# Attention of the later token blocks: two chunks a stop, inside an output pass, through the free h bank

## The chip, the cores and the metric

One core of one Trainium2 chip. The metric is the device time of one execution in microseconds (us). The engines go by the profile's names: PE (TensorE), DVE (VectorE), ACT (ScalarE), POOL (GpSimd), SP (SyncE, which issues the DMAs). PEld is PE's weight load.

## The reference

Attention with decay runs over blocks of 64 rows and carries a state; its output is the input of two MLPs in a row, each a product, a non-linear function and a second product.

```python
for b in range(nb):                       # 12 blocks of 64 rows
    intra = einsum('bhic,bhjc->bhij', qb, kb) * Dmask      # lam**(i-j), below the diagonal
    intra = einsum('bhij,bhjd->bhid', intra, vb)
    inter = einsum('bhid,bhde->bhie', qb * lam_pow, kv_state)
    out[:, :, sl] = intra + inter
    kv_state = lam_block * kv_state + einsum('bhsd,bhse->bhde', kb * rev_pow, vb)
# x = out as 1536 tokens x 512
x = elu(x @ w_in) @ w_out                 # d_ff = 2048, first MLP ("layer 0")
h = x @ w_in2; g = P(h) / (Q(h) + 1e-6)   # P cubic, Q = 1 + |b0||h| + |b1|h*h
y = g @ w_out2                            # second MLP ("layer 1")
```

The shapes are 2 batches, 8 heads, 768 rows, 64 columns a head.

## The kernel before, in words

The 1536 tokens are three token blocks t of 512, and each layer runs over them with d_ff in 16 steps f of 128. A step has an h pass (`mlp_h`, 12 matmuls of 128x512 at L435 into a PSUM bank of the pool `ph`, which has two) and, two steps later, a y pass (`mlp_y`, 12 matmuls at L517 into the four y banks of `py`). The 12 are three parts of four: high weights by high data, high weights by low data, low weights by high data. Between h and y stand the ELU's operations: ACT L448 and L449, DVE L450 (which is the last to read the h bank), ACT L452 (high part) and DVE L453 (low part). PSUM has eight banks: two `pa`, two `ph`, four `py`.

During t = 0 of layer 0 the weights of later steps are made from raw bits as well: DVE L78, L81 and L84 (1024 wide) put a weight tile together, ACT L127 rounds it to its high part and DVE L128 makes the low part. The raw tiles come by DMA (SP L122, L114).

The attention of the first 512 rows is done in the opening. Chunks 8 to 23, 64 rows of each of the 8 heads (4 pairs m), belong to token blocks 1 and 2 and are worked off in stops, 9 during t = 0 and 8 during t = 1 (the table `visits`), each between an h pass and the y pass that follows. At a stop (`att_visit`) `sm_products(n, d)` issues for the new chunk n the products of keys and queries (L340, into half 0 of bank `aa0`), and for the chunk before, d, the products of masked scores and values (L345, into `aa1`), of keys and values (L351, into half 1 of `aa0`) and of queries and state (L356, into `aa1`). All are 64x64, two for each pair m. Behind them: DVE L376 masks the scores of n, POOL L371 decays its queries (256 wide), ACT L384 copies the output of d to `xr`, DVE L388 adds the state (ACT L386 for a batch's first chunk), and in the step after ACT decays the state (L395, four operations) and the keys (L365, four). The powers of the decay for one chunk are made at the first stop (PE L333, ACT L335). The keys and values of a chunk are loaded by four DMAs (L323) and queries and keys of two chunks by two (L308).

In this part the program's order is written by hand (`manual_schedule`): every engine works its instructions in the order in which the loop over the steps emits them. From t = 2 on a scheduler orders them.

Of the kernel before, what the change touches and what calls it, by code (L numbers as in the profile page):

```python
# [8 lines left out]
F32 = mybir.dt.float32  # L9
# [7 lines left out]
P = 128  # L17
T = 512
# [11 lines left out]
def fused_kernel(ctx, tc, lam, qkv, w1, w2, ab, out):  # L30
# [16 lines left out]
    ph = ctx.enter_context(tc.tile_pool(name="ph", bufs=2, space=PSUM))  # L47
# [252 lines left out]
    aa_tiles = []  # L300

    def sm_load_qk(k):

        c, row = k // 2, 4 * P
        qk = qq.tile([P, NP, 2, C], F32, tag="qk", name=f"qk{c}")
        src = qkv[c, 0, 0]
        for rho, r in enumerate(ROWS):
            nc.sync.dma_start(  # L308
                out=qk[r].rearrange("p (g a) x i -> p g (a x i)", a=2),
                in_=bass.AP(src.tensor, src.offset + (1 - rho) * D * row,  # L310
                            [[row, D], [2 * P * row, NP // 2], [1, row]]))
# [15 lines left out]
    def sm_products(n, d):  # L327

        if not aa_tiles:
            aa_tiles.extend(pa.tile([P, T], F32, tag=f"pa{i}", name=f"aa{i}")  # L330
                            .rearrange("p (x m i) -> p x m i", x=2, m=NP) for i in range(2))
            for r in ROWS:
                nc.tensor.matmul(aa_tiles[1][r, 1], lhsT=pick[r], rhs=mask64[r, :, 1:CS + 1],  # L333
                                 start=True, stop=True, skip_group_check=True)
            nc.scalar.activation(out=qpow[:, :, 0:CS], in_=aa_tiles[1][:, 1], func=AF.Copy)  # L335
        pn, pd = chunk.get(n), chunk.get(d)
        for m in range(NP):
            if pn:
                for r in ROWS:
                    nc.tensor.matmul(aa_tiles[0][r, 0, m], lhsT=pn["k"][r, m],  # L340
                                     rhs=pn["q"][r, m], start=True, stop=True,
                                     skip_group_check=True)
            if pd:
                for i, r in enumerate(ROWS):
                    nc.tensor.matmul(aa_tiles[1][ROWS[1 - i], 0, m], lhsT=pd["kv"][r, m, 1],  # L345
                                     rhs=pd["s"][r, m], start=m == 0, stop=d % KB == 0,
                                     skip_group_check=True)
        for m in range(NP):
            if pd and d % KB < KB - 1:
                for r in ROWS:  # L350
                    nc.tensor.matmul(aa_tiles[0][r, 1, m], lhsT=pd["kv"][r, m, 0],  # L351
                                     rhs=pd["kv"][r, m, 1], start=True, stop=True,
                                     skip_group_check=True)
            if pd and d % KB:
                for i, r in enumerate(ROWS):
                    nc.tensor.matmul(aa_tiles[1][ROWS[1 - i], 0, m], lhsT=state[r, m, 0],  # L356
                                     rhs=pd["q"][r, m], start=False, stop=True,
                                     skip_group_check=True)

    def sm_decay_k(n):  # L360

        kv = chunk[n]["kv"]
        if n % KB < KB - 1:
            for m in range(NP):
                nc.scalar.activation(out=kv[:, m, 0], in_=kv[:, m, 0], func=AF.Copy,  # L365
                                     scale=mask64[:, m, CS - 1:CS])

    def sm_decay_q(n):
        q = chunk[n]["q"]
        if n % KB:  # L370
            nc.gpsimd.tensor_tensor(out=q, in0=q, in1=qpow[:, :, 0:CS], op=ALU.mult)  # L371

    def sm_mask(n):
        b = chunk[n]
        b["s"] = s = ap_.tile([P, NP, CS], F32, tag="s", name=f"s{n}")
        nc.vector.tensor_tensor(out=s, in0=aa_tiles[0][:, 0], in1=mask64[:, :, 0:CS], op=ALU.mult)  # L376

    def sm_out(d):

        t, js = d * CS // T, slice(d * CS % T, d * CS % T + CS)  # L380
        if t not in xraw:
            xraw[t] = xr.tile([P, NP, T], F32, tag="xr", name=f"xr{t}")
        first, last = d % KB == 0, d % KB == KB - 1
        nc.scalar.activation(out=xraw[t][:, :, js], in_=aa_tiles[1][:, 0], func=AF.Copy)  # L384
        if first:
            nc.scalar.activation(out=state[:, :, 0], in_=aa_tiles[0][:, 1], func=AF.Copy)  # L386
        elif not last:
            nc.vector.tensor_tensor(out=state[:, :, 0], in0=aa_tiles[0][:, 1],  # L388
                                    in1=state[:, :, 1], op=ALU.add)

    def sm_decay_state(d):

        if d % KB not in (0, KB - 1):
            for m in range(NP):
                nc.scalar.activation(out=state[:, m, 1], in_=state[:, m, 0], func=AF.Copy,  # L395
                                     scale=qpow[:, m, CS - 1:CS])

# [102 lines left out]
    def mlp_y(layer, t, f):  # L500
# [27 lines left out]
    with ExitStack() as actx:  # L528
# [4 lines left out]
        qq = actx.enter_context(tc.tile_pool(name="qq", bufs=2))  # L533

# [20 lines left out]
        dmask = ac.tile([P, H, C + 1], F32, name="dmask")  # L555
        qpow = ac.tile([P, NP, C], F32, name="qpow")
        state = ac.tile([P, NP, 2, D], F32, name="state")

        mask64 = dmask.rearrange("p (m h) i -> p m h i", h=2)[:, :, 1, CS:]
# [8 lines left out]
        def make_qpow():  # L568
# [5 lines left out]
            def double(n):  # L574
# [4 lines left out]
        yy, hh = ((py, "y"),) * 2, ((ph, "h"),) * 2  # L579
        pp = (yy, hh, yy, yy, hh, yy, yy, ((ph, "h"), (pa, "pa0")))  # L580
# [4 lines left out]
        loads = [[(sm_load_qk, first), (sm_load_kv, first)], [(sm_load_kv, first + 1)],  # L585
                 [(sm_load_qk, first + 2)]]
        loads += [[(sm_load_kv, k + 1)] + [(sm_load_qk, k + 2)] * (k % 2 == 0 and k + 2 < end)
                  for k in range(first + 1, end - 1)]
        with tc.manual_schedule():
# [17 lines left out]
            for load, k in loads.pop(0):  # L607
                load(k)
# [43 lines left out]
            for h in range(5, H):  # L652
# [45 lines left out]
            nc.gpsimd.tensor_copy(  # L698
                out=mask64[ROWS[1]],
                in_=dmask.rearrange("p (m h) i -> p m h i", h=2)[ROWS[1], :, 0, 0:CS + 1])  # L700
# [3 lines left out]
        h_pool = lambda: (ph, "h")  # L704
# [8 lines left out]
        def att_visit(due, more):  # L713

            n = todo.pop(0) if more and todo else None
            d = due.pop() if due else None
            sm_products(n, d)
            if n is not None:
                sm_mask(n)
                sm_decay_q(n)  # L720
                due.append(n)
            if d is not None:
                sm_out(d)
                del chunk[d]

        with tc.manual_schedule():
            due = []
            next_d = []
# [6 lines left out]
            visits = [(3, 5, 7, 9, 10, 12, 13, 14, 15), (2, 4, 6, 8, 10, 12, 14, 15)]  # L735
            assert sum(park_at.values()) == len(parks)
            for layer, t, f in steps(0, 0) + steps(0, 1):
                if f == 0 and t:
# [3 lines left out]
                    for n in due:  # L742
                        sm_decay_k(n)
                new = mlp_h(layer, t, f, later=True)
                queue.append((layer, t, f))
                if t or f != 1:
                    run(old, 2)
                    for d in next_d:
                        sm_decay_state(d)
                    next_d = []  # L750
# [27 lines left out]
                if f in visits[t]:  # L778
                    att_visit(due, t == 0 or f < NF - 1)
                    next_d = list(due)  # L780
                    for n in due:
                        if f < NF - 1:
                            sm_decay_k(n)
# [9 lines left out]
                if loads and (f in visits[t][1 - t:] or t == 0 and f in (1, 2)):  # L793
                    for load, k in loads.pop(0):
                        load(k)
# [3 lines left out]
                if len(queue) > LAG:  # L799
                    mlp_y(*queue.pop(0))  # L800
# [10 lines left out]
    def h_pool():  # L811
        nh[0] += 1
        return ((ph, "h"), (ph, "h"), (pa, "pa0"), (pa, "pa1"))[nh[0] % 4]
# [89 lines left out]
```

## Time and profile before

| | us |
|---|---|
| median of three runs | 572.01 (571.96 to 572.03) |
| the profiled execution | 572.56 |
| its span, first to last instruction | 570.8 |
| PE busy | 564.6 (99%) |
| DVE busy | 464.7 (81%) |
| ACT busy | 358.5 (63%) |
| POOL busy | 29.8 (5%) |

The profiled execution lies 0.55 us above the median, and 1.8 us of it lie outside the span. PE is busy from end to end, so its column says little by itself. What is to be read is the chain of work that ended last, which gives the price of each pass and each stop, and the other engines' timelines in the stretch of the stops: which of them runs how far behind PE.

### The profile page before, as it was taken

How to read it: one execution, taken by the hardware profiler on the slowest of the kernel's cores; microseconds unless marked ns; L12 is line 12 of the kernel's file. 1: busy time of each engine (PE TensorE's matmuls, PEld its weight loads, DVE VectorE, ACT ScalarE, POOL GpSimd, SP SyncE). 2: the span in 40 equal slices, each digit the busy share in tenths (PEclk: the TensorE clock that was granted, in tenths of full speed). 3: DMA queues.
4: the chain of work that ended last, by engine and by line, in shares of the span. 5: the costliest groups of instructions: out<-in, count | busy, mean ns of one | idle time of the engine just before them, and what ended most of it. 6: DMA issues, size and time to landing. Idle time of an engine off the chain costs nothing.

```text
span 570.8 us, 9255 instructions
## 1 busy us (share of the span) xinstructions
PE 564.6 (99%) x3550; PEld 464.9 (81%) x3550; DVE 464.7 (81%) x722; ACT 358.5 (63%) x690; POOL 29.8 (5%) x51
## 2 busy tenths in 40 slices
PE   8999999999999999999999999999999999999997
PEld 7877888888888888888888888888888888888885
DVE  6999999965676635877979999888898888898882
ACT  3746646875554545555568976667877666776672
POOL 7401001100100000000000000000000000000000
PEclk9999999999999999999999999999999999999999
DMA  8977677464687513434432500000400000200001
GB/s 291 318 225 243 237 227 214 107 206 128 204 240 229 165 49 136 167 135 177 150 108 78 182 3 1 1 2 0 145 3 2 0 1 0 75 0 1 1 1 74
DMA packets 41215, 64.58 MB, mean 113 GB/s; under 512 B 20178, under 2 KB 20178, under 8 KB 41170
## 3 DMA queue, kind: packets, MB, share of 16 engines
q1 hardware_dynamic: 41168, 63.98, 35.8%
q8 instruction: 28, 0.46, 0.3%
q14 instruction: 17, 0.14, 0.1%
q10 hardware_dynamic: 2, 0.00, 0.0%
HBM read 53.48 MB, written 10.49 MB: 112 GB/s over the span
## 4 chain that ended last, share of the span: by engine, by line
PE 98%; DMA 1%; SPq 0%; ACT 0%; issue 0%
PE h L435 46%; PE y L517 43%; PE y L426 3%; PE aa L340 1%; DMA att<-qkv_in 1%; PE aa L351 1%; PE pa L243 1%; PE pa L209 1%; PE pa L249 0%; PE aa L356 0%; PE aa L345 0%; SPq L192 0%; PE sums L256 0%; PE pa L291 0%; ACT o L487 0%; PE aa L333 0%
## 5 line engine op out<-in xcount | busy, mean ns | idle before, releaser
L435 PE MATMUL h<-xhi,w 128*128 128x512 f32 x768 | 204.8, 389 | 0.0
L517 PE MATMUL y<-ghi,w 128*128 128x512 f32 x712 | 191.8, 392 | 0.0
L435 PEld LDWEIGHTS h<-xhi,w 128*128 128x128 f32 x768 | 143.8, 188 | 30.3 <-DVE w L128 0.4
L517 PEld LDWEIGHTS y<-ghi,w 128*128 128x128 f32 x712 | 132.3, 188 | 27.8
L435 PE MATMUL h<-xlo,w 128*128 128x512 f32 x384 | 102.6, 389 | 0.0
L517 PE MATMUL y<-glo,w 128*128 128x512 f32 x356 | 95.3, 389 | 0.0
L435 PEld LDWEIGHTS h<-xlo,w 128*128 128x128 f32 x384 | 72.1, 188 | 15.0
L517 PEld LDWEIGHTS y<-glo,w 128*128 128x128 f32 x356 | 66.8, 188 | 14.2
L461 ACT ACTIVATE a<-h,babs 128x512 f32<-128x512 f32 x48 | 33.0, 688 | 63.8 <-PE h L435 63.8
L448 ACT ACTIVATE a<-h 128x512 f32<-128x512 f32 x48 | 28.3, 589 | 43.1 <-PE h L435 42.9
L465 DVE SCALAR_TENSOR_TENSOR b<-b,babs,a 128x512 f32<-128x512 f32 x48 | 36.0, 751 | 20.9 <-ACT b L462 20.7
L450 DVE SCALAR_TENSOR_TENSOR b<-a,h 128x512 f32<-128x512 f32 x48 | 32.7, 681 | 15.3 <-ACT a L449 12.1
L452 ACT ACTIVATE ghi<-b 128x512 fp32r<-128x512 f32 x48 | 30.0, 626 | 22.4 <-DVE b L450 22.4
L453 DVE TENSOR_TENSOR glo<-b,ghi 128x512 fp32r<-128x512 f32 x48 | 34.0, 709 | 7.0 <-ACT ghi L452 4.8
L463 ACT ACTIVATE p<-h,cab 128x512 f32<-128x512 f32 x48 | 37.7, 785 | 0.0
L467 ACT ACTIVATE a<-b,one 128x512 f32<-128x512 f32 x48 | 35.0, 729 | 3.1 <-DVE b L465 2.6
L469 DVE SCALAR_TENSOR_TENSOR p<-p,cab,h 128x512 f32<-128x512 f32 x48 | 35.8, 746 | 1.2
L473 DVE SCALAR_TENSOR_TENSOR b<-b,one,a 128x512 f32<-128x512 f32 x48 | 35.8, 746 | 0.1
L475 DVE SCALAR_TENSOR_TENSOR p<-p,cab,a 128x512 f32<-128x512 f32 x48 | 35.8, 746 | 0.0
L58 DVE TENSOR_TENSOR glo<-p,ghi 128x512 fp32r<-128x512 f32 x48 | 33.0, 688 | 3.0 <-PE y L426 1.5
L468 DVE TENSOR_TENSOR p<-p,h 128x512 f32<-128x512 f32 x48 | 32.8, 682 | 2.9 <-ACT p L463 2.9
L477 DVE SCALAR_TENSOR_TENSOR p<-b,p 128x512 f32<-128x512 f32 x48 | 33.1, 690 | 1.2
(88 smaller groups left out, 611.2 us busy)
## 6 DMA issues: line engine op xcount, KB each, us to landing
raw<-w_in SPq DMA_DIRECT2D x64, 512.0 KB, 4.5
att<-qkv_in SPq DMA_DIRECT2D x16, 256.0 KB, 6.0
qk<-qkv_in SPq DMA_DIRECT2D x16, 256.0 KB, 4.3
kv<-qkv_in SPq DMA_DIRECT2D x64, 64.0 KB, 4.0
w2d<-wbuf SPq DMA_DIRECT2D x16, 256.0 KB, 4.5
wbuf<-w2d SPq DMA_DIRECT2D x16, 256.0 KB, 2.8
x2d<-o SPq DMA_DIRECT2D x12, 256.0 KB, 2.3
x2r<-x2d SPq DMA_DIRECT2D x12, 256.0 KB, 3.1
```

The costliest lines, as they stand in the source:

```text
L58: lo_eng.tensor_tensor(out=lo, in0=src, in1=hi.bitcast(F32), op=ALU.subtract)
L435: nc.tensor.matmul(h, lhsT=w[:, a, 0, k * P:(k + 1) * P], rhs=xs[layer, t, k][b], start=i == k == 0, stop=i == 2 and k == NP - 1)
L453: lambda: nc.vector.tensor_tensor(out=glo, in0=b, in1=ghi.bitcast(F32), op=ALU.subtract)]
L461: nc.scalar.activation(out=a, in_=h, func=AF.Abs, scale=babs[:, 0:1])
L463: nc.scalar.activation(out=p, in_=h, func=AF.Identity, scale=cab[:, 3:4], bias=cab[:, 2:3])
L465: nc.vector.scalar_tensor_tensor(out=b, in0=b, scalar=babs[:, 1:2], in1=a, op0=ALU.mult, op1=ALU.add)
L467: nc.scalar.activation(out=a, in_=b, func=AF.Ln, bias=one[:, 0:1])
L469: nc.vector.scalar_tensor_tensor(out=p, in0=p, scalar=cab[:, 1:2], in1=h, op0=ALU.add, op1=ALU.mult)
L473: nc.vector.scalar_tensor_tensor(out=b, in0=b, scalar=one[:, 0:1], in1=a, op0=ALU.add, op1=ALU.mult)
L475: nc.vector.scalar_tensor_tensor(out=p, in0=p, scalar=cab[:, 0:1], in1=a, op0=ALU.add, op1=ALU.mult)
L477: nc.vector.scalar_tensor_tensor(out=p, in0=b, scalar=2.0, in1=p, op0=ALU.subtract, op1=ALU.mult, reverse0=True)
L517: nc.tensor.matmul(ys[layer, t][m], lhsT=w[:, a, 1, m * P:(m + 1) * P], rhs=g[b], start=f == i == 0, stop=False)
```

## The change

- Nine stops in place of seventeen. The list `at` names the steps (s = 16 t + f): 3, 6, 9, 12, 14, 18, 22, 26, 30. A stop takes two chunks.
- A stop stands inside the y pass: `mlp_y` calls `between` behind its second part, so that eight matmuls of y come before the stop and four after it.
- Scores of two chunks fill `aa0` (L346). Outputs no longer go to `aa1` but to the spare h bank `ax` (L351, L366): the bank of tag h0 or h1 that the next step's h pass takes. Products of keys and values (L361, into `aa1`) run one chunk behind the scores, not two.
- Each operation behind the products is done once for two chunks: mask L388 (512 wide), decay of queries L380 on POOL (512 wide, for the first chunk of a batch too), copy of the outputs L397 on ACT (512 wide). States are added (L405, L407) and decayed (L414) for one chunk at a time, keys too (L375).
- The powers `pow64` are made in step f = 1 (`sm_banks`, L332 and L334). `mask64` and `pow64` become small tiles of their own (one more POOL copy, L736), the big tables move into a weight slot, keys and values have three buffers, and the order of a few loads on SP changes.

```diff
-        for m in range(NP):
-            if pd and d % KB < KB - 1:
-                    nc.tensor.matmul(aa_tiles[0][r, 1, m], lhsT=pd["kv"][r, m, 0],
+        if d is not None:
+            aa_x[0] = spare.rearrange("p (m x i) -> p m x i", x=2, m=NP)
+        for j in range(2):
+            pn = chunk.get(n + j) if n is not None else None
+            pd = chunk.get(d + j) if d is not None else None
...
+        for j in range(2):
+            c = n + j - 1 if n is not None else None
...
+        nc.gpsimd.tensor_tensor(
+            out=q, in0=q, in1=pow64.rearrange("p m (b i) -> p m b i", b=1)
+            .to_broadcast([P, NP, 2, CS]), op=ALU.mult)
...
+        nc.scalar.activation(out=xraw[t][:, :, js].rearrange("p m (b i) -> p m b i", b=2),
+                             in_=aa_x[0], func=AF.Copy)
...
-    def mlp_y(layer, t, f):
+    def mlp_y(layer, t, f, between=None):
...
+            if between and i == 1:
+                between()
...
+        at = [3, 6, 9, 12, 14, NF + 2, NF + 6, NF + 10, NF + 14]
...
+            spare = ph.tile([P, T], F32, tag=f"h{(f + 1) % 2}", name=f"ax{s}") if v else None
...
-            visits = [(3, 5, 7, 9, 10, 12, 13, 14, 15), (2, 4, 6, 8, 10, 12, 14, 15)]
...
-                    mlp_y(*queue.pop(0))
+                    mlp_y(*queue.pop(0), between=(lambda: att_visit(s, f)) if s in at else None)
```

ACT, steps 6 and 7 of t = 0, before (`w0_6` is the weight tile of step 6, `ghi` the high part of the ELU, `xr` the attention's output):

```order
L448 ACTIVATE a0_0_6_808<-h0_0_6_793 128x512
L449 ACTIVATE a0_0_6_808<-a0_0_6_808 128x512
L127 ACTIVATE w0_6_816<-w0_6_817 128x1024
L452 ACTIVATE ghi0_0_6_806<-b0_0_6_809 128x512
L448 ACTIVATE a0_0_7_856<-h0_0_7_841 128x512
L449 ACTIVATE a0_0_7_856<-a0_0_7_856 128x512
L384 ACTIVATE xr1_763<-aa1_613 128x4x64
```

The same place now:

```order
L466 ACTIVATE a0_0_6_796<-h0_0_6_781 128x512
L467 ACTIVATE a0_0_6_796<-a0_0_6_796 128x512
L127 ACTIVATE w0_6_804<-w0_6_805 128x1024
L397 ACTIVATE xr1_890<-ax6_825 128x4x128
L470 ACTIVATE ghi0_0_6_794<-b0_0_6_797 128x512
L414 ACTIVATE state_164<-state_164,pow64_163 128x64 x4
L466 ACTIVATE a0_0_7_923<-h0_0_7_908 128x512
```

The copy of the outputs has moved ahead of step 7's ELU, and it now reads the spare h bank, behind the weight tile of step 6 (L127).

DVE, steps 5 and 6 of t = 0, before (`raw0_6` holds the bits of the weight tile, `glo` the low part of the ELU):

```order
L453 TENSOR_TENSOR glo0_0_4_668<-b0_0_4_670,ghi0_0_4_667 128x512
L376 TENSOR_TENSOR s9_760<-aa0_612,dmask_158 128x256
L388 TENSOR_TENSOR state_160<-aa0_612,state_160 128x4x64
L81 SCALAR_TENSOR_TENSOR w0_5_722<-raw0_5_635,w0_5_722 128x1024
L84 SCALAR_TENSOR_TENSOR w0_5_722<-raw0_5_635,w0_5_722 128x1024
L450 SCALAR_TENSOR_TENSOR b0_0_5_718<-a0_0_5_717,h0_0_5_702 128x512
L78 TENSOR_SCALAR w0_6_817<-raw0_6_687 128x1024
L128 TENSOR_TENSOR w0_5_721<-w0_5_722,w0_5_721 128x1024
L453 TENSOR_TENSOR glo0_0_5_716<-b0_0_5_718,ghi0_0_5_715 128x512
L81 SCALAR_TENSOR_TENSOR w0_6_817<-raw0_6_687,w0_6_817 128x1024
L84 SCALAR_TENSOR_TENSOR w0_6_817<-raw0_6_687,w0_6_817 128x1024
```

The same stretch now, from the ELU of step 5 on:

```order
L468 SCALAR_TENSOR_TENSOR b0_0_5_745<-a0_0_5_744,h0_0_5_729 128x512
L78 TENSOR_SCALAR w0_6_805<-raw0_6_714 128x1024
L128 TENSOR_TENSOR w0_5_752<-w0_5_753,w0_5_752 128x1024
L471 TENSOR_TENSOR glo0_0_5_743<-b0_0_5_745,ghi0_0_5_742 128x512
L81 SCALAR_TENSOR_TENSOR w0_6_805<-raw0_6_714,w0_6_805 128x1024
L84 SCALAR_TENSOR_TENSOR w0_6_805<-raw0_6_714,w0_6_805 128x1024
L388 TENSOR_TENSOR s10_892<-aa0_529,mask64_162 128x512
L407 TENSOR_TENSOR state_164<-aa1_530,state_164 128x4x64
```

The operations on the weight tile, L78 to L84, stand in this order in both kernels; the mask of the stop now stands behind L84, and in step 5 there is no mask.

PE at the stop of step 5, before, its end and the y pass behind it (`state` by queries, then y):

```order
L351 MATMUL aa_612<-kv_203 64x64 x2
L356 MATMUL aa_613<-qk_200,state 64x64 x2
L351 MATMUL aa_612<-kv_203 64x64 x2
L356 MATMUL aa_613<-qk_200,state 64x64 x2
L517 MATMUL y_0_0_570<-ghi_0_3_599,w_3_605 128x512
L517 MATMUL y_0_1_571<-ghi_0_3_599,w_3_605 128x512
L517 MATMUL y_0_2_572<-ghi_0_3_599,w_3_605 128x512
L517 MATMUL y_0_3_573<-ghi_0_3_599,w_3_605 128x512
```

The last products of the stop stand ahead of all 12 matmuls of y. PE at the stop of step 6, now, its end and what follows (`ax` is the spare bank):

```order
L361 MATMUL aa_530<-kv_675 64x64 x2
L366 MATMUL ax_825<-qk_204,state 64x64 x2
L535 MATMUL y_0_0_581<-ghi_0_4_693,w_4_703 128x512
L535 MATMUL y_0_1_582<-ghi_0_4_693,w_4_703 128x512
L535 MATMUL y_0_2_583<-ghi_0_4_693,w_4_703 128x512
L535 MATMUL y_0_3_584<-ghi_0_4_693,w_4_703 128x512
L453 MATMUL h_0_7_908<-xhi_0_0_265,w_5_752 128x512 x2
```

Four matmuls of y stand between the stop and the h pass of step 7, whose bank is the one that `ax` held.

## Rows read from the trace of the kernel before

**Rows 1.** The page: busy time by engine, and the chain by engine.

```profile
PE 564.6 (99%) x3550; PEld 464.9 (81%) x3550; DVE 464.7 (81%) x722; ACT 358.5 (63%) x690; POOL 29.8 (5%) x51
...
PE 98%; DMA 1%; SPq 0%; ACT 0%; issue 0%
```

**Rows 2.** Chain of work, in order of time: start us, us, what.

```profile
36.16 0.46 PE aa L340 x16
...
45.01 2.95 PE h L435 x12
...
54.75 2.72 PE y L517 x12
57.47 2.72 PE h L435 x12
...
72.39 0.20 PE aa L340 x2
...
73.48 2.95 PE y L517 x12
76.43 2.72 PE h L435 x12
...
79.78 0.47 PE aa L356 x16
```

**Rows 3.** Timeline of DVE: start us, us, engine line op out<-in xcount [idle before <-releaser].

```profile
44.88 0.70 DVE L78 TENSOR_SCALAR w<-raw 128x1024 int32<-128x1024 int32 x1 [1.26 <-DMA raw<-w_in]
45.49 1.22 DVE L128 TENSOR_TENSOR w<-w,w 128x1024 fp32r<-128x1024 f32 x1
...
52.58 0.42 DVE L376 TENSOR_TENSOR s<-aa,dmask 128x256 f32<-128x256 f32 x1
52.92 0.42 DVE L388 TENSOR_TENSOR state<-aa,state 128x256 f32<-128x256 f32 x1
...
55.64 0.68 DVE L450 SCALAR_TENSOR_TENSOR b<-a,h 128x512 f32<-128x512 f32 x1
...
57.99 0.68 DVE L453 TENSOR_TENSOR glo<-b,ghi 128x512 fp32r<-128x512 f32 x1
58.60 1.22 DVE L81 SCALAR_TENSOR_TENSOR w<-raw,w 128x1024 int32<-128x1024 int32 x1
59.85 1.23 DVE L84 SCALAR_TENSOR_TENSOR w<-raw,w 128x1024 int32<-128x1024 int32 x1
60.99 0.68 DVE L450 SCALAR_TENSOR_TENSOR b<-a,h 128x512 f32<-128x512 f32 x1
```

**Rows 4.** Timeline of ACT.

```profile
58.20 0.58 ACT L448 ACTIVATE a<-h 128x512 f32<-128x512 f32 x1
...
61.11 1.06 ACT L127 ACTIVATE w<-w 128x1024 fp32r<-128x1024 f32 x1 [1.66 <-DVE w L84]
62.08 0.61 ACT L452 ACTIVATE ghi<-b 128x512 fp32r<-128x512 f32 x1
```

**Rows 5.** Groups by line: out<-in xcount | busy, mean ns | idle before.

```profile
L487 ACT ACTIVATE o<-y 128x512 f32<-128x512 f32 x24 | 13.3, 604 | 5.1 <-PE y L426 5.1
...
L575 POOL TENSOR_TENSOR qpow<-qpow 128x256 f32<-128x256 f32 x1 | 0.7, 727 | 0.0
L575 POOL TENSOR_TENSOR qpow<-qpow 128x128 f32<-128x128 f32 x1 | 0.4, 400 | 0.1
```

**Rows 6.** Timelines of POOL and DVE where POOL works beside DVE.

```profile
39.94 0.73 POOL L371 TENSOR_TENSOR qk<-qk,qpow 128x256 f32<-128x256 f32 x1 [19.71 <-ACT qpow L335]
40.05 1.70 DVE L81 SCALAR_TENSOR_TENSOR w<-raw,w 128x1024 int32<-128x1024 int32 x1
...
48.66 1.64 POOL L371 TENSOR_TENSOR qk<-qk,qpow 128x256 f32<-128x256 f32 x1 [7.99 <-PE aa L340]
...
73.10 1.15 POOL L371 TENSOR_TENSOR qk<-qk,qpow 128x256 f32<-128x256 f32 x1 [11.43 <-PE aa L340]
73.57 1.76 DVE L128 TENSOR_TENSOR w<-w,w 128x1024 fp32r<-128x1024 f32 x1
```

**Rows 7.** PE's last matmul, and windows behind it; PEclk (1.00 is full) before the DMA share.

```profile
566.46 0.39 PE L426 MATMUL y<-ghi,w 128*128 128x512 f32 x1
...
569.00:570.00 1.00, 0.00 (x0) 0.00 (x0) 0.00 (x0) 0.00 (x0) 0.00 (x0) 1.00 0.07 23
570.00:571.00 1.00, 0.00 (x0) 0.00 (x0) 0.00 (x0) 0.00 (x0) 0.00 (x0) 0.54 0.00 0
```

More of the change, by code (lines that the diff above doesn't have):

```diff
@@ L360, in sm_decay_k @@
     def sm_decay_k(n):
-        kv = chunk[n]["kv"]
-        if n % KB < KB - 1:
+        if n in chunk and n % KB < KB - 1:
+            kv = chunk[n]["kv"]
             for m in range(NP):
@@ L376, in sm_mask @@
-        nc.vector.tensor_tensor(out=s, in0=aa_tiles[0][:, 0], in1=mask64[:, :, 0:CS], op=ALU.mult)
+        s = ap_.tile([P, 2, NP, CS], F32, tag="s", name=f"s{n}")
+        for j in range(2):
+            chunk[n + j]["s"] = s[:, j]
+        nc.vector.tensor_tensor(
+            out=s, in0=aa_tiles[0], in1=mask64[:, :, 0:CS].rearrange("p (b m) i -> p b m i", b=1)
+            .to_broadcast([P, 2, NP, CS]), op=ALU.mult)
     def sm_out(d):
-        t, js = d * CS // T, slice(d * CS % T, d * CS % T + CS)
+        t, js = d * CS // T, slice(d * CS % T, d * CS % T + 2 * CS)
@@ L391, in sm_decay_state, with sm_state @@
-    def sm_decay_state(d):
-        if d % KB not in (0, KB - 1):
+        nc.scalar.activation(out=xraw[t][:, :, js].rearrange("p m (b i) -> p m b i", b=2),
+                             in_=aa_x[0], func=AF.Copy)
+    def sm_state(n):
+        if n - 1 in chunk and n % KB:
+            j = n % 2
+            if n % KB == 1:
+                nc.scalar.activation(out=state[:, :, j], in_=aa_tiles[1][:, j], func=AF.Copy)
+            else:
+                nc.vector.tensor_tensor(out=state[:, :, j], in0=aa_tiles[1][:, j],
+                                        in1=state[:, :, 2], op=ALU.add)
@@ L394, in sm_decay_state @@
+    def sm_decay_state(n):
+        if n % KB not in (0, KB - 1):
             for m in range(NP):
-                nc.scalar.activation(out=state[:, m, 1], in_=state[:, m, 0], func=AF.Copy,
-                                     scale=qpow[:, m, CS - 1:CS])
+                nc.scalar.activation(out=state[:, m, 2], in_=state[:, m, n % 2], func=AF.Copy,
+                                     scale=pow64[:, m, CS - 1:CS])
     xs = {}
@@ L584, in fused_kernel @@
         first, end = todo[0], todo[-1] + 1
[L585 to L588, printed above, removed]
+        at = [3, 6, 9, 12, 14, NF + 2, NF + 6, NF + 10, NF + 14]
+        pairs = list(range(first, end, 2))
+        loads = {}
+        for i, k in enumerate(pairs[1:]):
+            s0 = at[i] if i else 1
+            for j, load in enumerate(((sm_load_kv, k - 1), (sm_load_qk, k), (sm_load_kv, k))):
+                loads.setdefault(s0 + (j if i == 0 else j // 2), []).append(load)
+        loads.setdefault(at[-2], []).append((sm_load_kv, end - 1))
+        work, late, states = {}, {}, {}
+        for v, s in enumerate(at[:-1]):
+            k = first + 2 * v
+            if v:
+                late.setdefault(s - 1, []).append((sm_decay_k, k - 1))
+                work.setdefault(s, []).append((sm_decay_k, k))
+            work.setdefault(s + 1, []).append((sm_decay_state, k))
+            states[s + 1] = k + 1
+            work.setdefault(s + 2 + (s + 2 == NF), []).append((sm_decay_state, k + 1))
         with tc.manual_schedule():
@@ L606, in fused_kernel @@
             load_pair(1)
-            for load, k in loads.pop(0):
-                load(k)
+            for load in (sm_load_qk, sm_load_kv):
+                load(first)
             def s_part(i):
@@ L711, in fused_kernel, with att_visit @@
         queue = []
[L713 to L717, printed above, removed]
+        def att_visit(s, f):
+            v = at.index(s)
+            spare = ph.tile([P, T], F32, tag=f"h{(f + 1) % 2}", name=f"ax{s}") if v else None
+            n = pairs[v] if v < len(pairs) else None
+            d = pairs[v - 1] if v else None
+            sm_products(n, d, spare)
+            if d is not None:
+                sm_out(d)
             if n is not None:
@@ L720, in att_visit @@
                 sm_decay_q(n)
-                due.append(n)
             if d is not None:
-                sm_out(d)
-                del chunk[d]
+                if n is not None:
+                    sm_state(n)
+                for j in range(2):
+                    del chunk[d + j]
         with tc.manual_schedule():
-            due = []
-            next_d = []
             lows = w
@@ L747, in fused_kernel @@
                     run(old, 2)
[L748 to L750 removed]
+                    for op, n in work.get(s, ()):
+                        op(n)
                     now = []
@@ L777, in fused_kernel @@
                     att_hand(*atts[-1])
[L778 to L783, printed above, removed]
+                    sm_banks()
+                    sm_decay_k(first)
+                if s in states:
+                    sm_state(states[s])
+                for op, n in late.get(s, ()):
+                    op(n)
                 for w in now if t or f else ():
```

116 lines of the change are left out of this document (56 added, 60 removed).

## The prediction

> **What bounds the kernel now.** I read the page first: PE is busy 99% of the span and the chain of work lies on PE for 98% [rows 1]. So the time is the sum of PE's work, and the change can gain only by giving PE less, or lose by making it wait. Next the chain in order of time [rows 2]: a pass of 12 matmuls takes 2.72 us (h at 57.47, y at 54.75), the y pass behind a stop 2.95 (at 73.48), a stop 1.09 (72.39 to 73.48). A stop thus costs 1.09 + 2.95 - 2.72 = 1.32. Its sixteen 64x64 products of one kind take 0.47 (L356 alone at 79.78; L340 alone at 36.16, 0.46), and I call that a round: two kinds interleaved take one round, and a full stop has two. What is left, 1.32 - 2 x 0.47 = 0.38, is the overhead of changing from wide to small products and back.
>
> Then the other engines at the stops of t = 0, since they now make what PE will wait for. A DVE step without a stop is 5.35 us (L450 at 55.64, the next at 60.99), back to back [rows 3]; PE's step without a stop is 2 x 2.72 = 5.44. DVE is as full as PE there, and behind: the bits for the weight tile w4 came late at 44.88 (1.26 idle on the DMA), and nothing has made up for it since. ACT is behind too: the h pass that ended at 54.75 is read by L448 only at 58.20 [rows 4]. PE does not feel that, because an h bank has slack of a step.
>
> **The change part by part.** Every sum goes against the profiled execution, 572.56 us with a span of 570.8; it lies 0.55 above the median, and I carry the difference over to the median.
>
> 1. *Fewer stops.* 17 become 9: 8 x 0.38 = -3.04.
> 2. *More rounds.* By the code, before: one at the first stop, two at the 16 others, 33. After: three at the first stop, four at each of seven, and four at the last (two of scores by values, two of queries by state): 35. That is +0.94. That a change inside a y pass costs no more than one between h and y is an assumption: the same wide and small products alternate.
> 3. *The wait of h5* for the low weights of w3. The chain shows this pass at 2.95 without a stop behind it [rows 2], 0.23 over 2.72; its L128 begins at 45.49 [rows 3], set by the late bits. In the new order the first stop, at step 3, has two rounds more and so delays h5 by 0.94, which covers the wait: -0.23.
> 4. *Powers* moved from the first stop to step 1, states and keys decayed for one chunk at a time as before, loads and the POOL copy moved: PE does the same products elsewhere, the DMAs land ahead of use, DVE and ACT save some halves of operations. I take 0; ACT's early decay of the keys of chunk 8 in step 1 could cost 0 to 0.3.
> 5. *The new wait.* The output of a stop stands in the spare h bank, and the next h pass is the next but four matmuls on PE. So PE waits for ACT's copy L397, and with PE in order everything behind that h pass waits. Before, the copy L384 read `aa1`, which nothing needed for a step. What does L397 wait for at step 6? On ACT it stands behind L127 of w6, which needs DVE's L84 of w6.
>
>    When is L84 through? Before, L78 of w4 began at 44.88, when its bits had come, and L84 of w6 at 59.85 [rows 3], with no idle between. The bits come no earlier now. Of this stretch's operations only the mask L376 is gone (0.34, from 52.58 to 52.92; the state's addition, 0.33, stays). L84 of w6 begins at 59.51 and ends, 1.23 long, at 60.74.
>    L127 follows 0.03 later (61.11 after 61.08) and ACT's next operation 0.97 behind it (62.08) [rows 4]: L397 starts at 61.74. It copies 128x512 from PSUM; the nearest row, L487, takes 0.604 [rows 5]: 62.34, and 0.05 for the hand-over, 62.4.
>    When could PE start h7? Before at 57.47 [rows 2]. In front of it stood two stops with three rounds; now two stops with seven, and no wait of h5: 57.47 + 4 x 0.47 - 0.23 = 59.12. **PE waits 62.4 - 59.1 = 3.3 us.**
>
> 6. *POOL's decay of the queries*, twice as wide. L371 (256 wide) takes 0.73 undisturbed. While it runs, a DVE operation on SBUF data is stretched: L81 from 1.22 to 1.70 at 40.05, L128 from 1.23 to 1.76 at 73.57; at 48.66 POOL waited instead, 1.64 in all, and DVE lost nothing, since what followed read PSUM [rows 6]. The cost is the overlap less 0.15 (POOL was done at 40.67, 0.62 after 40.05: 0.48). At 512 wide I estimate 0.727 + 2 x (0.727 - 0.400) = 1.38, by the two widths of L575 [rows 5]. When is POOL ready at step 6? y4 begins at 54.75 + 0.94 - 1.32 - 0.23 = 54.14; two thirds of it are through at 55.95; the two rounds of scores end at about 57.1. DVE is then in L128 of w5, until 57.65 (57.99 - 0.34), and next comes L453's successor L471, on SBUF data. POOL takes its turn at 57.65, and DVE, which lies on the path to L84 of w6, loses 1.38 - 0.15 = 1.2. The bounds are 0 (as at 48.66) and 1.2; I take 1.2, because the operation that stands next is of the kind that was stretched. **Wait of PE: 4.5.**
>    The Trainium skill, "SBUF — State Buffer", section "Who interferes with whom", calls the port pair that DVE and GpSimd share an exclusive lock: a DVE operation with two SBUF inputs contends with a GpSimd one that reads SBUF, one with a single SBUF input does not. The rows above agree (1.76 against 1.23). By that rule L471 is held and the wait is 4.5, without it 3.3.
>
> 7. *The other stops of t = 0.* Once PE has lost 4.5, DVE and ACT have caught up by as much. At step 9 L84 of w9 ends at 60.74 + 1.2 + 3 x 5.35 + 0.6 (wide mask) + 2 x 0.33 = 79.3, L397 at 80.9; PE would want the bank after h7 at 63.6, six passes and a stop (0.38 + 4 x 0.47 = 2.26) later, at 82.2. Margin 1.3, or 0.1 if POOL holds DVE again. Stops 12 and 14 stand in a stretch with weights in halves, whose margins I cannot work out that closely: 0 to 1 each, 0 taken. In t = 1 ACT has no such weight tiles, and four y matmuls (some 0.94) stand against a copy of 0.6: 0.
>
> Sum: -3.04 + 0.94 - 0.23 + 4.5 = **+2.2 us**, so 574.8 for the profiled execution, 574.2 against the median of 572.01. The gain of 2.3 is real and is paid back twice by one wait.
>
> **The rivals.**
>
> *PE's clock falls during the wait.* PE's last matmul ended at 566.46 + 0.39; with PE idle the granted clock stood at 1.00 (2.4 GHz) through the window 569 to 570 and came to a mean of 0.54 in the next, so near 1.2 GHz [rows 7]. A wait of PE could bring the same. The trace has no row of the way back; I bound the price by 0 and one pass at half rate, 2.72 more: up to 576.9. Against it: in the window 569 to 570 PE had been idle for over 2 us and the clock was still full, so a wait of 3.3 or 4.5 may end before it falls.
> The Trainium skill, "TensorE: Matmul & The Clock Gate", Part 1, says that idleness halves the rate to 1.2 GHz and sustained work restores it; rows 7 agree with the first half, and no row here shows the second.
>
> *The wait without POOL's part.* DVE gets in first, and 3.3 remains: -2.33 + 3.3 = +1.0, 573.0.
>
> *More stops wait*, at 9, 12 or 14, by 0.5 to 2 in all beside the 4.5: 574.7 to 576.2; say 575.5.
>
> *No wait: the other side, faster.* ACT's copy comes before PE needs it: then only items 1 to 3 count, 572.0 - 2.3 = 569.7. For this L84 of w6 would have to end by about 57.4, so that L127 (0.97) and the copy (0.60) are through by 59.1: 3.3 us earlier than the 60.74 above. The bits of w4 would have to land that much sooner, or the bits not be what DVE waits for. Their issue is not moved, and behind 44.88 DVE has no idle time to lose; I see little for it. That the change leaves the stops where they were is excluded by the order of PE's instructions.
>
> **How the numbers follow.** Forecast, wait with POOL's part: 0.42, 574.2. Clock falls: 0.20, 576 to 577. Without POOL's part: 0.20, 573.0. More stops wait: 0.10, 575.5. No wait: 0.08, 569.7. A measurement of this kernel tells 0.2%, 1.14 us, from no change. The case at 573.0 lies just inside that bound and spreads over it: half of it counts as same, with a little of the forecast's own lower end, so same is 0.13; faster is 0.08; slower 0.79. The range of 8 in 10 leaves out the case without a wait and the tail of the clock's: 572.4 to 577.0.
>
> **What would show it.** Right: in the profile of the changed kernel the chain has one piece on ACT at 59 to 63 us, the h pass of step 7 starts near 63.6, PE idles 3 to 5 us in front of it with ACT's copy of the spare bank as releaser, and that copy stands behind L127 with DVE's L84 behind that. DVE's L471 or its neighbour there is 1.2 longer than 0.68. Every other stop costs 2.26 on the chain, and behind t = 1 the passes lie as before. Wrong: no idle time on PE at 59 us, or L127 of w6 well before 60; a second gap of the same size at step 9, 12 or 14; small products that take more than 0.47 a round inside a y pass; a granted clock under 1.00 about 62 to 66 us.

## The result and the profile after

| | before | changed |
|---|---|---|
| median, us | 572.02 (571.92 to 572.45, 6 runs) | 577.04 (575.59 to 577.82, 6 runs) |
| ratio | | 1.0084, 95% interval 1.0069 to 1.0099 |
| profiled execution, us | 572.56 | 577.45 |
| its span, us | 570.8 | 575.7 |
| mean granted clock | 0.999 | 0.994 |

The changed kernel is slower by 0.84%. The runs of before lie within 0.5 us of each other, those of the changed kernel within 2.2: something in it differs from one execution to the next, and the mean granted clock differs with it (0.993 to 0.997).

The page of the changed kernel, busy time and the chain by engine (beside [rows 1]):

```profile
PE 565.4 (98%) x3550; PEld 467.5 (81%) x3550; DVE 464.7 (81%) x714; ACT 359.2 (62%) x682; POOL 27.6 (5%) x45
...
PE 90%; DVE 5%; DMA 2%; issue 1%; ACT 1%; SPq 0%; DVEq 0%
```

PE runs the same 3550 matmuls, but 8% of the chain has left it, most of it to DVE. The waits of the changed kernel (engine, line, what was waited for: us in total, times, longest) name the one place:

```profile
PE h L453 <- ACT xr L397: 5.4, 1, 5.4
```

The chain of the changed kernel around it, start us, us, what (beside [rows 2]):

```profile
49.80 6.88 DMA raw<-w_in
...
57.38 2.31 DVE w L128
59.70 0.60 DVE glo L471
60.30 1.15 DVE w L81
61.47 1.24 DVE w L84
62.73 1.06 ACT w L127
63.78 0.49 ACT xr L397
64.32 4.90 PE h L453 x12
...
80.12 1.81 PE y L535 x8
81.94 0.20 PE aa L346 x2
...
83.96 1.12 PE y L535 x4
85.08 2.73 PE h L453 x12
```

Read upwards from 64.32: the h pass of step 7 waits for the copy L397 out of the spare bank, which stands behind the rounding L127, which waits for DVE's L84. So the chain of the prediction is there, link for link. The next stop (81.94 to 85.08 with the rest of y) shows what a stop costs when nothing is late: the products, the last four matmuls of y and the h pass take 2.02 + 1.12 + 2.73, where these matmuls of y and h alone take 0.91 + 2.72. The stop costs 2.24.

DVE and POOL of the changed kernel at the same place (beside [rows 3, 6]):

```profile
44.23 0.69 DVE L78 TENSOR_SCALAR w<-raw 128x1024 int32<-128x1024 int32 x1
...
56.78 0.69 DVE L78 TENSOR_SCALAR w<-raw 128x1024 int32<-128x1024 int32 x1 [1.43 <-DMA raw<-w_in]
57.38 2.31 DVE L128 TENSOR_TENSOR w<-w,w 128x1024 fp32r<-128x1024 f32 x1
...
56.99 1.63 POOL L380 TENSOR_TENSOR qk<-qk,pow 128x512 f32<-128x512 f32 x1 [16.30 <-PE ax L351]
```

L128 is stretched from 1.23 to 2.31 while POOL's wide operation runs, and before it DVE waits 1.43 us for the bits of w6. In the kernel before, L78 of w6 had no idle time ahead of it:

```profile
56.24 0.69 DVE L78 TENSOR_SCALAR w<-raw 128x1024 int32<-128x1024 int32 x1
```

The granted clock of the changed kernel in windows (PE's busy time is the first number behind the length; PEclk stands before the DMA share), beside [rows 7]:

```profile
59.00:60.00 1.00, 0.00 (x0) 0.00 (x0) 1.00 (x2) 0.00 (x0) 0.00 (x0) 1.00 0.14 45
...
61.00:62.00 1.00, 0.00 (x0) 0.00 (x0) 0.96 (x2) 0.00 (x0) 0.00 (x0) 0.77 0.00 0
62.00:63.00 1.00, 0.00 (x0) 0.00 (x0) 1.00 (x2) 0.27 (x1) 0.00 (x0) 0.50 0.00 0
...
68.00:70.00 2.00, 2.00 (x10) 1.59 (x9) 1.25 (x2) 0.71 (x2) 0.00 (x0) 0.91 0.98 228
```

It falls to 0.50 (1.2 GHz) while PE waits, and is back at full some 4 us after PE has started again at 64.32; the h pass of step 7 takes 4.90 us in place of 2.72.

The stretch behind t = 0 is as forecast. From the last y pass of t = 0 to that of t = 1 before, and then in the changed kernel:

```profile
123.82 2.72 PE y L426 x12
...
221.41 2.72 PE y L426 x12
```

```profile
130.42 2.72 PE y L444 x12
...
226.58 2.72 PE y L444 x12
```

97.59 us before, 96.16 now: t = 1 gains 1.43 us. The changed kernel is 6.60 us behind at the end of t = 0 (130.42 against 123.82), so all that is lost is lost by then.

### The profile page after: what moved, and what is told of

It is laid out like the page before. It is cut to its first block, busy times and chain, and to the rows that moved or that the text cites. A ratio compares the mean times of both kernels' runs of the same rounds, so it can differ in the third digit from the quotient of the medians.

```text
span 575.7 us, 9228 instructions
## 1 busy us (share of the span) xinstructions
PE 565.4 (98%) x3550; PEld 467.5 (81%) x3550; DVE 464.7 (81%) x714; ACT 359.2 (62%) x682; POOL 27.6 (5%) x45
## 4 chain that ended last, share of the span: by engine, by line
PE 90%; DVE 5%; DMA 2%; issue 1%; ACT 1%; SPq 0%; DVEq 0%
PE h L453 42%; PE y L535 40%; PE y L444 3%; DVE w L81 1%; DMA raw<-w_in 1%; DVE w L128 1%; DVE w L84 1%; PE aa L346 1%; PE pa L243 1%; DMA att<-qkv_in 1%; PE pa L209 1%; PE aa L361 1%; DVE glo L471 1%; PE ax L366 0%; DVE w L78 0%
## 5 line engine op out<-in xcount | busy, mean ns | idle before, releaser
L471 DVE TENSOR_TENSOR glo<-b,ghi 128x512 fp32r<-128x512 f32 x48 | 32.9, 686 | 9.3 <-ACT ghi L470 7.1
```

What stands on the lines that cost most here:

```text
L471: lambda: nc.vector.tensor_tensor(out=glo, in0=b, in1=ghi.bitcast(F32), op=ALU.subtract)]
```

## The experiments

Each was timed beside the kernel before on the same chip, and the ratio is to that; the chips of different rows differ, so rows are compared by their ratios. "Wait" is PE's longest wait for the copy in the profiled execution, "clock" the range of mean granted clocks over the runs of the kernel.

| kernel | median, us | ratio, 95% interval | wait, us | clock |
|---|---|---|---|---|
| changed | 577.04 | 1.0084 (1.0069 to 1.0099) | 5.4 | 0.993 to 0.997 |
| e1: copy first at step 6 | 576.40 | 1.0086 (1.0053 to 1.0118) | 4.0 | 0.994 to 0.997 |
| e7: at 6, 9, 12 | 575.49 | 1.0053 (1.0037 to 1.0069) | 1.9 | 0.997 to 1.000 |
| e12: at 6, 9, 12, 14 | 572.97 | 1.0013 (1.0000 to 1.0025) | not known | 0.999 to 1.000 |
| e11: POOL held back alone | 576.60 | 1.0076 (1.0054 to 1.0098) | 3.8 | 0.993 to 1.000 |
| e10: both | 569.99 | 0.9961 (0.9948 to 0.9973) | none | 0.999 to 1.000 |
| e2: no decay at 6 | 574.42 | 1.0051 (1.0034 to 1.0068) | 3.0 | 0.993 to 1.000 |
| e3: no decay at 3, 6 | 575.46 | 1.0053 (1.0035 to 1.0071) | 2.7 | 0.993 to 1.000 |
| e8: e7, no decay at 3, 6, 9 | 574.88 | 1.0043 (1.0028 to 1.0058) | 1.9 | 0.997 to 1.000 |
| e9: seven L81 less | 576.28 | 1.0059 (1.0040 to 1.0079) | 2.0 | 0.993 to 1.000 |
| e4: e1, copy made 4 times | 574.11 | 1.0050 (1.0026 to 1.0074) | 3.0 | 0.996 to 1.000 |
| e5: e1, copy made 8 times | 576.95 | 1.0094 (1.0072 to 1.0115) | 4.3 | 0.993 to 0.996 |
| e6: stop ahead of y | 579.82 | 1.0122 (1.0103 to 1.0141) | 3.5 | 0.994 to 1.000 |

The profiled execution of e12 took 2008 us, with passes of 9.9 us, so the row of e12 is of the nine others and its waits are not known. The medians of e3, e4, e5, e6 and e11 lie above every time that was expected for them.

### The copy ahead of the rounding, at step 6 (e1)

```diff
                 for w in now if t or f else ():
-                    run(w, len(w) - 1)
+                    run(w, len(w) - 1 - (s == 6))
...
+                if s == 6:
+                    run(lows, 1)
```

> The changed kernel with one move: at the stop of step 6, ACT copies the outputs out of the spare h bank (L397) before it rounds the weight tile of step 6 (L127), not behind it. Theory (the wait is ACT's order: the copy stands behind L127, which stands behind DVE's L84): PE's wait of 5.4 us in front of the h pass of step 7 falls to 0.3 or less, the granted clock stays at 1.00, the h pass takes 2.72 again, and the time is 572.0 - 2.3 = 569.7 us, at most 1 us more if the weight tiles of steps 6 and 7 now come late for PE. Rival (a late bank is only the place where DVE's lateness shows, and it would show at the next pass that needs a weight tile): the wait moves to the h passes of steps 8 and 9, 2 to 4 us there, and the time stays at 572 or above.

The time stays. ACT at step 6, then the chain at step 9:

```profile
59.77 0.58 ACT L397 ACTIVATE xr<-ax 128x512 f32<-128x512 f32 x1
64.38 1.06 ACT L127 ACTIVATE w<-w 128x1024 fp32r<-128x1024 f32 x1 [4.02 <-DVE w L84]
```

```profile
82.74 1.06 ACT w L127
83.80 0.49 ACT xr L397
...
84.34 2.08 PE h L453 x4
```

The theory held at its place: the copy no longer waits for L84, and the h pass of step 7 starts without a gap that counts. But I had taken the lateness of DVE as something that the wait at step 6 cures and that would otherwise be harmless. It isn't cured if PE doesn't wait: at step 9 the copy stands behind L127 of w9, and PE waits 4.0 us there. The rival was right that the wait moves, but it moved to the next copy, not to a weight tile.

### Without POOL's decay of the queries at step 6 (e2), and at 3 and 6 (e3)

```diff
-                sm_decay_q(n)
+                if s not in (6,):
+                    sm_decay_q(n)
```

> The changed kernel without POOL's decay of the queries at the stop of step 6 (this part of the result is left out). Theory (POOL's operation holds DVE on the path to L84): L128 at that place takes 1.2 again in place of 2.3, and PE's wait falls from 5.4 to 4.3 us; with the clock's price unchanged at 2.2 the time is about 575.9 us, with the clock untouched 573.8. Rival (POOL is beside the path, the late bits of the weight tile set it): the wait stays at 5.4 and the time at 577.

> The changed kernel, ACT's order as it is, without POOL's decay of the queries at steps 3 and 6 (left out of the result). Without the one at step 6 PE's wait in the profile was 3.0 to 3.5 us in place of 5.4. Theory (each of POOL's operations costs DVE 1.1 us on the path to L84): the wait falls by 1.1 more, to about 2.1 us, clock 1.00, and the time is 569.7 + 2.1 = 571.8 us. Rival (the first is swallowed by DVE's wait for the bits of a weight tile): 3.0 to 3.5 us as without the one, 573 to 574.5.

Without the decay at step 6 the wait fell from 5.4 to 3.0 us, by more than POOL's 1.1: in this execution DVE also waited less for the bits of w6. Without both it is 2.7, where 2.1 was expected. DVE's L78 of w6 in the two, and in the run with nothing but seven L81 less (e9, below):

```profile
55.54 0.69 DVE L78 TENSOR_SCALAR w<-raw 128x1024 int32<-128x1024 int32 x1 [0.32 <-DMA raw<-w_in]
```

```profile
54.89 0.69 DVE L78 TENSOR_SCALAR w<-raw 128x1024 int32<-128x1024 int32 x1 [0.45 <-DMA raw<-w_in]
```

So the bits and POOL's operation are both on the path. The single times of e3 go with the clock: 571.71 in the one execution with a mean clock of 1.00, near what the sum without the clock said (571.8), and 574.1 to 577.6 in the nine others at 0.993 to 0.997. The spread of 5.9 us is more than the clock cost in any profiled execution (2.8), so the waits must differ too; of the nine, one was profiled.

### A wait of known length (e4, e5)

```diff
-                sm_out(d)
+                for _ in range(4 if s == 6 else 1):
+                    sm_out(d)
```

> As the run with the copy ahead of L127, but at the stop of step 6 ACT makes the copy four times in a row, so that PE waits for a known time that has nothing to do with DVE: copies from about 58.0 on, 0.56 apart, the last ends near 60.3, PE is ready at 58.95: wait 1.3 us. Theory (the clock falls only in a long wait): clock 1.00, time 569.7 + 1.3 = 571.0 us. Rival (any wait of PE costs the clock): 1 to 2.7 us more, 572 to 573.7.

> The same with eight copies: the last ends near 62.5, wait 3.6 us. If the clock holds: 569.7 + 3.6 = 573.3 us. If it falls as in the changed kernel, the h pass of step 7 takes 4 to 5 us in place of 2.72: 574.5 to 575.5. The changed kernel waited 5.4 and paid 2.2 for the clock.

With eight copies PE waited 4.3 us at step 7 for ACT alone, and paid as the changed kernel did:

```profile
62.96 5.43 PE h L453 x12
```

2.71 us over a pass, in a wait that DVE has no part in: the price belongs to PE's idle time, not to its cause. With four copies the first wait (2.0 us in this execution) cost no clock, but neither the theory (571.0) nor the rival (up to 573.7) fits the median of 574.11: the time was lost at step 9, as in e1, with 3.0 us of wait and this pass behind it, 1.88 over 2.72:

```profile
83.08 4.60 PE h L453 x12
```

The price isn't a function of the wait's length alone. The profiled execution of e2 waited 3.0 us and kept its clock (first fence: PE idle in the first window, PEclk 1.00 in both); that of e9 waited 2.0 us and lost it, and there it fell after PE had started again at 61.0 (second fence):

```profile
60.00:62.00 2.00, 0.01 (x1) 0.01 (x1) 2.00 (x5) 1.61 (x3) 0.00 (x0) 1.00 0.26 70
62.00:64.00 2.00, 2.00 (x9) 1.63 (x10) 2.00 (x3) 1.51 (x5) 0.00 (x0) 1.00 1.01 373
```

```profile
60.00:62.00 2.00, 0.96 (x4) 0.82 (x5) 2.00 (x5) 2.00 (x6) 0.00 (x0) 1.00 0.78 236
62.00:64.00 2.00, 2.00 (x8) 1.58 (x7) 2.00 (x4) 0.56 (x3) 0.00 (x0) 0.64 1.06 364
64.00:66.00 2.00, 2.00 (x6) 1.52 (x6) 0.74 (x1) 0.65 (x2) 0.00 (x0) 0.51 0.81 216
```

The three profiled executions with waits of 4.0 us and more (changed, e1, e5) paid 2.2 to 2.8 us over the pass behind the wait. Of the eight whose longest wait was 1.9 to 3.8, six paid 1.5 to 1.9 (e3, e4, e7, e8, e9, e11) and two 0.3 (e2, e6: passes of 3.06 and 3.01, at full clock). What decides between them the runs don't show. They do show that the mean clock differs from one execution to the next of the same kernel, and the times spread with it.

### The stop ahead of y (e6)

```diff
-                    mlp_y(*queue.pop(0), between=(lambda: att_visit(s, f)) if s in at else None)
+                    if s in at:
+                        att_visit(s, f)
+                    mlp_y(*queue.pop(0))
```

> The changed kernel with every stop ahead of its y pass, between h and y as before, not inside it. PE then has 12 matmuls of y behind the stop, not 4: 1.8 us more to cover the wait for the copy. Theory: the wait in front of the h pass of step 7 falls from 5.4 to 3.6 us; a second one of 0 to 1 us appears ahead of the products into the spare bank, which waits for the ELU of the h pass before; 573.5 to 575.5 us. Rival (a stop inside y is what costs, by more than two changes between wide and small products): waits as in the changed kernel but 1 to 2 us less in the stops, so 575 with 5.4 us of wait still there.

PE's weight loads with the idle time before them:

```profile
55.45 0.14 PEld L351 LDWEIGHTS ax<-s,kv 64*64 64x64 f32 x2 [1.53 <-DVE b L468]
64.19 0.77 PEld L453 LDWEIGHTS h<-xhi,w 128*128 128x128 f32 x4 [3.89 <-ACT xr L397]
...
85.06 0.76 PEld L453 LDWEIGHTS h<-xhi,w 128*128 128x128 f32 x4 [2.15 <-ACT xr L397]
```

The wait for the copy fell to 3.5 to 3.9 as expected, and a second one of 1.5 us came ahead of it, in front of the spare bank, where 0 to 1 was expected; so nothing was gained at step 6. The wait of 2.15 at step 9 and one of 1.1 at the first stop of t = 1, again in front of the spare bank, came on top; with them it is the slowest of all, though its profiled execution kept the full clock. That is what the place inside y is for: eight matmuls of y ahead of the stop cover the ELU that still reads the bank, four behind it cover the copy, and both must be covered. The rival, that a stop inside y costs more, falls: where nothing waits a stop costs 2.23 to 2.29 in the changed kernel, and 2.24 to 2.26 here, between h and y.

### The copy ahead of the rounding at 6, 9 and 12 (e7), and without POOL's decay too (e8)

```diff
-                    run(w, len(w) - 1 - (s == 6))
+                    run(w, len(w) - 1 - (s in (6, 9, 12)))
...
-                if s == 6:
+                if s in (6, 9, 12):
                     run(lows, 1)
```

> The changed kernel with ACT's copy ahead of the rounding L127 at the stops of steps 6, 9 and 12, not at step 6 alone. The run that did it at step 6 only took the wait away there (none at the h pass of step 7) and found it again at step 9, 4 us long, behind L127 of w9: DVE stays behind PE as long as PE doesn't wait. Theory (only the copy's place behind a weight tile makes PE wait; the tiles themselves are needed two steps later and are in time): no wait over 0.8 us, clock 1.00, 569.7 to 570.7 us, faster than both kernels. Rival (DVE is too late for the tiles as well): waits of 1 to 4 us on L127 or L128 at the h passes of steps 8 to 11, 572 us or more.

> The run before, without POOL's decay of the queries at steps 3, 6 and 9 (this part of the result is left out). Theory (DVE's lateness no longer touches PE once the copies are in front): the same time as the run before within 0.5 us. If waits on weight tiles of up to 0.8 us remain there, they go: 569.7. Rival (POOL's hold on DVE is what costs): over 1 us less than the run before.

The chain of e7:

```profile
112.50 0.63 ACT w L127
113.13 0.49 ACT xr L397
113.67 4.44 PE h L453 x12
```

The wait moved on to the last stop of t = 0, step 14, where the copy again stands behind a rounding, one of half width. The waits for weight tiles came to 0.6 us in all; with the copies of steps 6 and 9, three weight loads were 0.4 to 0.6 us late each before step 14. So the theory, no wait over 0.8 us, falls, and the rival's place was wrong as well. e8 waits at the same place for as long, although it had some 3 us less of POOL (three operations that stretch DVE by 1.1 each): DVE waited earlier on, 0.94 and 1.73 us, for the bits of w4 and w6. As a test of POOL it says that POOL's hold alone isn't what makes DVE late.

### Seven operations of DVE less (e9)

```diff
+        if 3 <= f <= 9:
+            del ops[1]
```

> The changed kernel, its orders as they are, with DVE's L81 left out for the weight tiles of steps 3 to 9 (their values are then not the weights): seven times 1.25 us of DVE's work less, on the path to L84. Theory (in t = 0 DVE is full, and what PE gains there DVE can't follow; PE's waits are DVE's lateness): the waits in front of the h passes go, clock 1.00, and the time is 572.0 - 2.3 = 569.7 us. Rival (the late bits of the weight tiles, so the DMAs, or the small products themselves set it): a wait of 2 us or more stays at step 6 and the time at 572 or above.

```profile
54.76 0.69 DVE L78 TENSOR_SCALAR w<-raw 128x1024 int32<-128x1024 int32 x1 [2.88 <-DMA raw<-w_in]
...
57.10 2.30 DVE L84 SCALAR_TENSOR_TENSOR w<-raw,w 128x1024 int32<-128x1024 int32 x1
```

The theory in its simple form falls: with 3.75 us less work up to there DVE came to w6 early and waited 2.88 for its bits, which had been asked for at 46.89, when the buffer came free, and L84 was stretched by POOL again. PE waited 2.0 us at step 6 and nowhere else in t = 0; the stops of 9, 12 and 14 were in time. So without that work the bits set the pace up to step 6, by a buffer's way round: DVE's L84 frees it, the DMA fills it (asked for at 46.89, used at 54.76), DVE takes it again. That behind step 6 DVE itself is what is late fits this run, which waits there no more, and e1 and e7, which do.

### POOL held back (e11), all four copies first (e12), and both (e10)

e10 as a diff to the changed kernel (`made[0]` is the weight tile that DVE puts together in this step); e11 has the first two pieces alone, e12 the last two:

```diff
+        made[0] = w
...
     def sm_decay_q(n):
+        if made[0] is not None and n < 16:
+            nc.gpsimd.tensor_copy(out=gate, in_=made[0][:, 1, DM - 1:DM])
...
-                    run(w, len(w) - 1)
+                    run(w, len(w) - 1 - (s in (6, 9, 12, 14)))
...
+                if s in (6, 9, 12, 14):
+                    run(lows, 1)
```

> The changed kernel with ACT's copy ahead of the rounding at the stops of steps 6, 9, 12 and 14, and with POOL's decay of the queries at steps 3, 6, 9 and 12 held until DVE's L84 of that step is through (a POOL copy of one column of the weight tile stands in front of it), so that it runs beside DVE's mask and state additions, which read PSUM. With the copies in front at 6, 9 and 12 alone PE waited at step 14, behind L127 of that step. Theory (DVE's lateness is the cause, POOL adds 1.1 us to it per stop): L128 and L471 at the stops take their 0.68 to 1.23 us, no wait over 0.8 us, 569.7 to 571 us, faster than before. Rival (DVE is so late that PE waits for the weight tiles or the ELU instead): waits of 1 to 3 us on L127, L128 or L468, 572 to 575 us.

> The changed kernel with POOL's decays at steps 3, 6, 9 and 12 held until DVE's L84 is through, ACT's order as it is (the copy behind the rounding). With both changes the time was 569.99 us, PE without a wait, and L84 of w6 was through at 59.6. Theory (two causes add up: DVE's lateness and the copy's place): the copy then ends near 61.3, PE is ready at 58.8: wait 2 to 2.5 us, and with the clock's price of 0 to 2.7 the time is 572 to 574.5. Rival (POOL's hold alone makes the wait): no wait, 570.

> The changed kernel with the copy ahead of the rounding at steps 6, 9, 12 and 14, without the hold on POOL. With the copies in front at 6, 9 and 12 alone PE waited about 0.8 us in all up to step 12 and 2 to 2.5 us at step 14. Theory (the copy's place decides, DVE's lateness alone is bearable): waits of 1 us or less in all, 570 to 571.5 us. Rival (DVE's lateness reaches PE in another way at step 14 or after, through the keys' decay on ACT, the weight tiles or the attention's split at the start of t = 1): 1.5 to 3 us of wait there, 572 us or more.

e10 comes to 569.99 us, within 0.3 of the sum without a wait, and is faster than both kernels. POOL, DVE and ACT of e10 at step 6:

```profile
59.68 0.18 POOL L382 COPY gate<-w 128x1 f32<-128x1 f32 x1 [16.40 <-DVE w L84]
59.82 1.30 POOL L384 TENSOR_TENSOR qk<-qk,pow 128x512 f32<-128x512 f32 x1
```

```profile
58.32 1.22 DVE L84 SCALAR_TENSOR_TENSOR w<-raw,w 128x1024 int32<-128x1024 int32 x1
59.46 0.68 DVE L392 TENSOR_TENSOR s<-aa,mask 128x512 f32<-128x512 f32 x1
60.06 0.41 DVE L411 TENSOR_TENSOR state<-aa,state 128x256 f32<-128x256 f32 x1
60.40 0.68 DVE L472 SCALAR_TENSOR_TENSOR b<-a,h 128x512 f32<-128x512 f32 x1
```

```profile
57.69 0.60 ACT L401 ACTIVATE xr<-ax 128x512 f32<-128x512 f32 x1 [0.33 <-PE ax L368]
59.58 1.06 ACT L127 ACTIVATE w<-w 128x1024 fp32r<-128x1024 f32 x1 [1.29 <-DVE w L84]
```

POOL runs its 1.30 beside three DVE operations that each read PSUM, and none of them is longer than elsewhere (0.68, 0.41, 0.68). The hold isn't perfect: at steps 3 and 9 POOL still met one operation on SBUF data (L78 took 1.06 for 0.69, L128 1.52 for 1.21). ACT waits for the copy's data instead of PE for the copy. With the changed kernel these make four combinations of two changes. The hold alone leaves 3.8 us of wait, where 2 to 2.5 was expected (the bits of w6 came 1.59 late for DVE in that execution, and the copy is behind the rounding), 576.60. The copies alone give 572.97 at full clock, as its rival said (572 or more); at what place PE waits there is not shown. By the ratios, the copies' place is worth 6.6 us with POOL held, and POOL's hold 3.0 us with the copies in place. Without the copies in place the hold gains nothing clear of the noise (1.0076 against 1.0084).

## Why the prediction was right, and where its sizes were off

The forecast was 574.2, slower, in a range up to 577.0, and the median is 577.04 (572.01 x 1.0084 = 576.8). The direction, the place and the chain behind the wait were right. The size was not: it lies at the upper edge of the range, 2.6 us over the forecast, and is that of the rival with the clock, which was forecast at 576 to 577 and had a chance of 0.20.

1. *Fewer stops, more rounds, h5 (items 1 to 3, -2.33):* right in sum. t = 1 gained 1.43, where 8 x 1.32 less 4 x 2.26 is 1.52, and e10, which doesn't wait, came out 2.1 us under the kernel before on its chip. A stop cost 2.23 to 2.29, where 2.26 was forecast. h5's part alone is not shown.
2. *When PE could start h7 (59.12):* 64.32 less the idle time of 5.36 in front of it is 58.96.
3. *L84 of w6 (item 5, begins 59.5, with POOL 60.7):* it began at 61.47. Two of its steps were off, with opposite signs, so that it came so near is in part luck. "The bits come no earlier now" was wrong: those of w4 were no hindrance at 44.23, 0.65 before the 44.88 that the sum starts from. Those of w6, which had been there in time before, were 1.43 late. Their two DMAs, asked for at nearly the same time (49.73 before, 49.42 now), took a median of 4.5 us to land before and 6.4 now. The chunk's keys and values are under way beside them (they are now asked for from 44.85 on, before from 56.66), but no run moves them, so that they are the cause is not shown. I had held the DMAs as landing ahead of use (item 4).
4. *POOL (item 6, 1.2):* right in kind and size, 2.31 for 1.23, but POOL started earlier (56.99, not 57.65) and it was L128 that was held, not L471. e10 shows the other half, that operations that read PSUM aren't touched. That an operation with a single SBUF input isn't held, as I put it, is not so for L78: beside POOL it took 1.31 in e4, 1.50 in e6 and 1.06 in e10 for 0.69.
5. *The copy behind L127 (item 5):* right; L127 starts 0.03 behind L84, and from L127 at 62.73 to PE at 64.32 it is 1.59, where 0.97 + 0.60 + 0.05 = 1.62 was forecast.
6. *The wait (4.5):* 5.4, 0.9 more: L84 began 0.8 later than forecast, and PE was ready 0.2 earlier.
7. *The clock, the first rival (0 to 2.72):* it fell, one of the signs that I had named for being wrong, and cost 2.18. It is most of what the forecast lacks, a term that was left at nothing in the sum and given too small a chance. The row on which I set "may end before it falls" was a single one, of the kernel's end; of the profiled executions with a wait of 1.9 us or more eight of the experiments lost it, and e2 and e6 did not.
8. *The other stops (item 7, none):* right for the changed kernel, and for the reason given, that the wait at 6 lets DVE and ACT catch up. I didn't draw the other half from it: take the wait away and it comes back at 9, then at 14 (e1, e7).

In sum, -2.33 for items 1 to 3 and -0.16 for the earlier h7, + 5.36 + 2.18 = +5.05; the spans differ by 4.9.

The rival "no wait", 569.7, is what the kernel does with the two orders of e10: 569.99.

## What to carry to other kernels

When an output moves into a bank that the next pass of the busiest engine needs, the copy out of it becomes urgent, and whatever stands ahead of it in the copying engine's queue becomes urgent with it: put the copy first, at every place, not only where the profile shows the wait, because here the engine that was late stayed late until somebody waited for it. Where an operation stretches another engine's work on the path, as POOL's does DVE's, it can be made to wait for the end of that work and run beside operations that it doesn't stretch. And a wait of PE has a price besides its own length: the waits of 1.9 to 5.4 us here cost another 0.3 to 2.8 us in the pass behind them.

## What the runs showed of the hardware that was not expected

- The granted clock fell in profiled executions with PE idle for 1.9 us (e7: 114 to 118 at 0.73 and 0.50, after a wait for the copy at step 14) and stayed full in two with 3.0 and 3.5 us (e2, e6). In e7 and e9 it fell after PE was at work again. It came back 3.0 us (e11) to 5.6 us (e1) after PE had started again, most of that at half rate.
- The wait and its price vary between executions of one kernel: e3 took 571.71 us at a mean clock of 1.00 and up to 577.60 at 0.994.
- The two DMAs of w6's bits took a median of 4.5 us from issue to landing in the kernel before and 6.4 in the changed one, with loads of keys and values under way beside them. This was seen together; no run parts the two.
- POOL's wide operation stretched DVE's L128, which reads two SBUF tiles, from 1.23 to 2.31 us, and L78, which reads one, from 0.69 to as much as 1.50 (e6). Operations that read PSUM took their usual time beside it (e10).
